# Loads and stores issued by GpSimd, one batch transposed on TensorE, and corrected DMA times in the plan of a fused attention and MLP kernel

## The chip, the cores and the metric

The kernel runs on one core of a Trainium2 chip. The metric is the time on the device in microseconds (us), the median of several runs.

Engines are named as the profile names them: PE is TensorE's matmul stream and PEld its weight loads, DVE is VectorE, ACT is ScalarE, POOL is GpSimd, SP is SyncE. A "q" after a name (SPq, POOLq) means that engine's instruction queue, here the issuing of DMAs. The "granted clock" is the share of TensorE's full clock that the chip allowed in a stretch (1.00 is all of it). PSUM is the memory that TensorE writes its results to; it is used in banks, and to "evict" a bank is to copy it out so that TensorE can write it again. "L301" is line 301 of the kernel; the change adds three lines, so L298 before is L301 after.

## The reference

Eight batches of cosine-weighted linear attention (8 heads, 576 tokens, head width 64), then a two-layer MLP with the gate h·cos(h) on all 4608 tokens:

```python
def phi(x, c, s):
    r = np.maximum(x, 0.0)
    return np.concatenate([r * c, r * s], axis=-1)
q_p = phi(q, cos_w, sin_w)
k_p = phi(k, cos_w, sin_w)
kv  = np.einsum('bhsf,bhsd->bhfd', k_p, v)
z   = np.sum(k_p, axis=2)
num = np.einsum('bhsf,bhfd->bhsd', q_p, kv)
den = np.einsum('bhsf,bhf->bhs', q_p, z)[..., None] + 1e-06
x   = num / den            # then to tokens x 512
h   = x @ w_in             # 512 -> 2048
out = (h * np.cos(h)) @ w_out   # 2048 -> 512
```

## The kernel before

The kernel records every operation as a step of a `Plan`: engine, occupied time, latency, the data it reads and writes. A list scheduler then runs the plan once with these assumed times and emits the steps in order of their planned start. The numbers in the plan thus set the order of each engine's instructions; the engines themselves run them in the order given. A DMA's assumed time is its bytes over a rate, on one shared "wire":

```python
nbytes, rate = s["dma"]
begin = max(free[e] + 1.3, wire)
wire = begin + nbytes / rate
done[n] = wire + 0.7
...
return [st[n] for n in sorted(order, key=lambda n: (st[n]["start"], n))]
```

Each batch is loaded with six DMAs, all issued by SyncE, into one raw tile per input:

```python
def load(b, nm, due, hs=(slice(0, H),)):
    ...
        def go5(h=h, five=five):
            nc.sync.dma_start(out=blocks(m, n)[:, h], in_=five)
        def go4(h=h, four=four):
            nc.sync.dma_start(out=blocks(m, 1 - n)[:, h, 0:NT, :], in_=four)
        pl.add("SP", 0.62, 0, due, go5, (), [(x, n) for x in part],
               dma=(nb * (NT + 1) / 1e3, 330.0))
        # ... and the same for go4
```

The "preps" turn raw q and k into relu(x)·cos on DVE and relu(x)·sin on ACT. There is one buffer `qp`, with one slot for each of five token tiles. From batch 2 on a DMA transpose, issued by SyncE, reads each slot and writes `qT`; the prep of the next batch may overwrite the slot only when that transpose has read it. The attention result x goes the same way (`xT<-x`). Batches 0 and 1 are transposed on TensorE (`q_pe`, `x_pe`).

```python
qp = sb("qp", [P, NT + 1, H, 2, D])        # one buffer, no second copy
...
def q_dma(b, t, due):
    dst, dkey = qdst(b, t)
    pl.add("SP", 0.62, 0, due, lambda: nc.sync.dma_start(
        out=dst, in_=qp[:, t].rearrange("p h g d -> p (h g d)"), transpose=True),
        [("qp", t, g, h) for g in range(2) for h in range(H)], [dkey],
        dma=(262.0, 200.0))
```

The MLP runs per chunk of 512 tokens: layer 1 into four PSUM banks (`M1`), the gate on ACT (`ch`) and DVE (`gT`), layer 2 into two banks (`M2`), evicted by ACT into `ost`, then stored:

```python
act(0.5, due, lambda O=O, t=t, m=m: nc.scalar.activation(
    out=O[:, t % 2, :], in_=M2[m], func=AF.Copy), [("M2", m)], [("ost", o, t % 2, 0)])
...
def put(dst, s, keys, q=nc.sync, eng="SP", nb=256.0):
    pl.add(eng, 0.62, 0, due + 1.0, lambda: q.dma_start(out=dst, in_=s), keys, [],
           dma=(nb, 330.0))
```

The main loop weaves a batch's attention between the layers of the chunk before it:

```python
for c in range(2, NC):
    if c < B:
        attention(c)
    layer2(c - 1)
    layer1(c)
```

## Time and profile before

| | before |
|---|---|
| median time | 351.63 us (3 runs, 350.76 to 352.52); 351.75 with the later run |
| span of the profiled run, granted clock | 348.6 us, 0.992 |
| PE busy | 292.8 us |
| PE idle in 68–204 us | about 22 us |
| DMA transposes of q, issue to landing | median 3.5, longest 7.0 us |

The page of the kernel before, its parts 1 and 4. Part 1 is busy time, share of the span and instruction count for each engine; part 4 is the chain of work that ended last, by engine and by line.

```profile
span 348.6 us, 5319 instructions
...
PE 292.8 (84%) x2032; PEld 154.1 (44%) x2032; DVE 181.0 (52%) x387; ACT 179.2 (51%) x290; POOL 7.9 (2%) x19
...
PE 57%; ACT 19%; DVE 12%; issue 6%; DMA 4%; SPq 0%; DVEq 0%; ACTq 0%
PE M L436 28%; PE M L412 20%; ACT ch L368 10%; DVE gT L370 10%; PE M L395 5%; DMA qm<-in_q_dram 4%; ACT ost L448 4%; ACT qp L233 2%; PE ATT L257 2%; PE ATT L319 1%; DVE x L329 1%; ACT V L246 1%; PE M L288 1%; ACT kp L233 1%; ACT qT L292 0%
```

PE is the busiest engine and holds most of the chain. DMA has 4% of it, two loads of q that start at 3.6 and 60.5 us.

The waits of PE in the kernel before, from 60 to 205 us: what ended the idle time, us in total, times, longest.

```profile
PE M L412 <- DVE gT L370: 9.0, 14, 1.3
PE M L395 <- DVE gT L370: 4.2, 3, 2.0
PE M L436 <- ACT ost L448: 3.9, 6, 0.7
...
```

PE's waits are short: a PSUM bank that the gate has not freed, or (L436) layer 2 waiting for an eviction, never over 0.7 us.

The instructions of line L298 (the DMA transposes of q) in the kernel before: issue duration in ns as min/median/max, then the time from issue to landing.

```profile
L298 SPq DMA_TRANSPOSE qT<-qp x30: 1232/1259/4068, 70.9 to 229.8; - x30
...
DMA to landing us min/median/max: 3.0/3.5/7.0
```

SyncE's timeline in the kernel before, a part of 143 to 160 us: start, duration, what was issued.

```profile
143.75 0.67 SPq L213 DMA_DIRECT2D km<-in_k_dram  x1
144.51 1.26 SPq L358 DMA_TRANSPOSE xT<-x  x1
145.94 3.76 SPq L298 DMA_TRANSPOSE qT<-qp  x2
...
```

Loads and transposes stand in one queue, one after another, with hardly a pause. That crowding is what the change sets out to relieve.

### The profile page before, as it was taken

The page shows a single profiled execution, that of the slowest core. Times are in us where ns is not written, and L with a number is a line of the kernel's source. Part 1 is how long each engine was busy: PE and PEld are TensorE (multiplying, and loading weights), DVE is VectorE, ACT ScalarE, POOL GpSimd, SP SyncE. Part 2 cuts the span into 40 slices and gives each one's busy share as a digit, 9 for nine tenths or more (in the row PEclk, how much of TensorE's full clock was granted, in tenths as well). Part 3 has the DMA queues.
Part 4 walks back from the last instruction along what each step waited for, and adds up shares of the span by engine and source line. Part 5 has one row for each costly group of instructions (what it writes and reads, how often), then busy time and mean ns, then how long its engine had stood idle before and what let it go on. Part 6 is the DMA issues. An engine that isn't in the chain of part 4 may idle for free.

```text
span 348.6 us, 5319 instructions
## 1 busy us (share of the span) xinstructions
PE 292.8 (84%) x2032; PEld 154.1 (44%) x2032; DVE 181.0 (52%) x387; ACT 179.2 (51%) x290; POOL 7.9 (2%) x19
## 2 busy tenths in 40 slices
PE   0478899676888779878988998999999999999983
PEld 0466646565543335433433453545444444444331
DVE  2646546967844667566666663643464333333300
ACT  2845558777553664564755665344433443443311
POOL 0430000000000000000000000000000000000000
PEclk9989999999999999999999999999999999999998
DMA  6999958999999989798494641561041010101111
GB/s 211 246 224 210 220 194 275 318 286 222 227 223 273 330 141 280 232 208 203 135 270 137 107 107 30 127 116 60 1 117 68 16 60 0 62 0 60 60 62 60
DMA packets 80217, 53.87 MB, mean 155 GB/s; under 512 B 48832, under 2 KB 77760, under 8 KB 80192
## 3 DMA queue, kind: packets, MB, share of 16 engines
q1 hardware_dynamic: 75520, 49.17, 53.3%
q0 software_dynamic: 4224, 4.19, 7.3%
q8 instruction: 16, 0.26, 0.3%
q10 hardware_dynamic: 448, 0.17, 0.2%
q14 instruction: 9, 0.07, 0.1%
HBM read 36.74 MB, written 9.44 MB: 132 GB/s over the span
## 4 chain that ended last, share of the span: by engine, by line
PE 57%; ACT 19%; DVE 12%; issue 6%; DMA 4%; SPq 0%; DVEq 0%; ACTq 0%
PE M L436 28%; PE M L412 20%; ACT ch L368 10%; DVE gT L370 10%; PE M L395 5%; DMA qm<-in_q_dram 4%; ACT ost L448 4%; ACT qp L233 2%; PE ATT L257 2%; PE ATT L319 1%; DVE x L329 1%; ACT V L246 1%; PE M L288 1%; ACT kp L233 1%; ACT qT L292 0%
## 5 line engine op out<-in xcount | busy, mean ns | idle before, releaser
L370 DVE TENSOR_TENSOR gT<-M,ch 128x512 f16<-128x512 f32 x144 | 98.2, 690 | 110.1 <-ACT ch L368 53.9
L368 ACT ACTIVATE ch<-M,PIH 128x512 f32<-128x512 f32 x144 | 96.6, 686 | 112.5 <-DVE gT L370 83.3
L436 PE MATMUL M<-w_out_sb,gT 128*128 128x512 f16 x576 | 141.0, 379 | 11.4 <-ACT ost L448 10.9
L412 PE MATMUL M<-xT,w_in_sb 128*128 128x512 f16 x384 | 94.7, 378 | 11.7 <-DVE gT L370 9.0
L436 PEld LDWEIGHTS <-gT 128*128 128x128 f16 x576 | 54.6, 97 | 76.7 <-issue 18.1
L412 PEld LDWEIGHTS <-w_in_sb 128*128 128x128 f16 x448 | 43.2, 97 | 68.2 <-issue 21.1
L395 PE MATMUL M<-xT,w_in_sb 128*128 128x256 f16 x256 | 30.4, 272 | 8.3 <-DVE gT L370 6.5
L448 ACT ACTIVATE ost<-M 128x512 f32<-128x512 f32 x35 | 20.6, 592 | 32.1 <-PE M L436 32.1
L395 PEld LDWEIGHTS <-w_in_sb 128*128 128x128 f16 x256 | 24.6, 97 | 13.1 <-issue 6.8
L233 ACT ACTIVATE kp<-km,CS 128x512 f16<-128x512 f32 x40 | 26.2, 712 | 4.9 <-DMA km<-in_k_dram 4.9
L233 ACT ACTIVATE qp<-qm,CS 128x512 f16<-128x512 f32 x39 | 26.2, 713 | 2.7 <-DMA qm<-in_q_dram 2.7
L236 DVE TENSOR_SCALAR kp<-km,CS 128x512 f16<-128x512 f32 x40 | 16.6, 481 | 11.3 <-DMA km<-in_k_dram 6.7
L329 DVE TENSOR_TENSOR x<-ATT,rec 128x512 f16<-128x512 f32 x30 | 20.6, 688 | 0.6
L319 PEld LDWEIGHTS <-qT 128*128 128x128 f16 x320 | 15.0, 101 | 10.1 <-issue 4.5
L236 DVE TENSOR_SCALAR qp<-qm,CS 128x512 f16<-128x512 f32 x41 | 18.1, 476 | 1.8 <-DMA qm<-in_q_dram 1.8
L288 PE MATMUL M<-IDENT,qp 128*128 128x128 f16 x72 | 6.3, 258 | 12.2 <-ACT qp L233 12.2
L412 PE MATMUL M<-xR,w_in_sb 128*128 128x512 f16 x64 | 16.4, 379 | 0.0
L319 PE MATMUL ATT<-kvz,qT 128*128 128x65 f16 x272 | 13.7, 195 | 2.0 <-DVE x L329 2.0
L249 DVE CAST V<-vm 128x512 f16<-128x512 f32 (+1 forms) x42 | 14.2, 382 | 0.0
L257 PE MATMUL ATT<-V,kp 128*128 128x65 f16 x320 | 11.8, 194 | 1.7 <-DVE V L249 1.0
L257 PEld LDWEIGHTS <-kp 128*128 128x128 f16 x320 | 11.1, 98 | 3.8 <-DVE V L249 1.2
L288 PEld LDWEIGHTS <-qp 128*128 128x128 f16 x80 | 6.2, 117 | 13.0 <-ACT qp L233 12.4
(38 smaller groups left out, 58.7 us busy)
## 6 DMA issues: line engine op xcount, KB each, us to landing
out_dram<-ost SPq DMA_DIRECT2D x32, 256.0 KB, 2.8
km<-in_k_dram SPq DMA_DIRECT2D x8, 640.0 KB, 5.3
qm<-in_q_dram SPq DMA_DIRECT2D x8, 640.0 KB, 5.7
km<-in_k_dram SPq DMA_DIRECT2D x8, 512.0 KB, 6.1
qm<-in_q_dram SPq DMA_DIRECT2D x8, 512.0 KB, 6.7
vm<-in_v_dram SPq DMA_DIRECT2D x6, 640.0 KB, 4.9
vm<-in_v_dram SPq DMA_DIRECT2D x6, 512.0 KB, 5.9
w_in_sb<-in_moe_w_in_dram POOLq DMA_DIRECT2D x4, 512.0 KB, 9.4
```

Of the source, the lines that this page charges most:

```text
L233: act(0.2 + 0.37 * f, due, lambda: nc.scalar.activation(out=out_, in_=in_, func=AF.Relu, scale=sc), rd, wr)
L236: dve(0.09 + 0.28 * f, due, lambda: nc.vector.tensor_scalar(out=out_, in0=in_, scalar1=0.0, scalar2=sc, op0=ALU.max, op1=ALU.mult), rd, wr)
L257: nc.tensor.matmul(ATT[:, hb, hh * D1:(hh + 1) * D1], lhsT=kp[:, t, h].rearrange("p g d -> p (g d)"), rhs=V1[b % 2][:, t, h, :], start=(t ...
L288: nc.tensor.matmul(ps[:, h, :], lhsT=qp[:, t, h].rearrange("p g d -> p (g d)"), rhs=IDENT, is_transpose=True)
L319: nc.tensor.matmul(A[:, hb, hh * D1:(hh + 1) * D1], lhsT=a[:, h, :], rhs=z[:, h, :], start=(i == 0), stop=(i == len(parts) - 1))
L329: dve(0.62, due, lambda: nc.vector.tensor_tensor(out=x16[n].rearrange("p (b h) d -> p b h d", b=2), in0=N[:, :, :, 0:D], in1=rec[n].rearra ...
L368: act(0.59, due, lambda: nc.scalar.activation(out=ch[c], in_=bank, func=AF.Sin, bias=PIH, scale=1.0), [key, "PIH"], [("ch", c)])
L370: dve(0.61, due, lambda: nc.vector.tensor_tensor(out=dst, in0=bank if len(dst.shape) == 2 else bank.rearrange("p (j s) -> p j s", j=dst.sh ...
L395: nc.tensor.matmul(M1[m][:, jj * 2 * P:(jj + 1) * 2 * P], lhsT=w_in_sb[:, cc, j * P:(j + 1) * P], rhs=X[:, cc, ts], start=(cc == 0), stop= ...
L412: nc.tensor.matmul(M1[m], lhsT=w_in_sb[:, cc, j * P:(j + 1) * P], rhs=X[:, cc, :], start=(cc == 0), stop=(cc == NCT - 1))
L436: nc.tensor.matmul(M2[m], lhsT=G[:, j, t * P:(t + 1) * P], rhs=w_out_sb[:, j, :], start=(j == 0), stop=(j == NJT - 1))
L448: act(0.5, due, lambda O=O, t=t, m=m: nc.scalar.activation(out=O[:, t % 2, :], in_=M2[m], func=AF.Copy), [("M2", m)], [("ost", o, t % 2, 0)])
```

## The change

The intent: give SyncE only the DMA transposes, let the mostly idle GpSimd (busy 7.9 of 348.6 us) issue loads and stores from batch 2 on, take the transposes of batch 2 (and x of batch 3) from the DMA engines, and put the measured durations of transposes and loads into the plan. The core of the diff, with cuts:

```diff
+    Q_PE, X_PE = (2,), (2, 3)
...
-            def go5(h=h, five=five):
-                nc.sync.dma_start(out=blocks(m, n)[:, h], in_=five)
+            queue, eng, occ = (nc.sync, "SP", 0.65) if b < 2 else (nc.gpsimd, "POOL", 0.95)
+
+            def go5(h=h, five=five, queue=queue):
+                queue.dma_start(out=blocks(m, n)[:, h], in_=five)
...
-            pl.add("SP", 0.62, 0, due, go5, (), [(x, n) for x in part],
-                   dma=(nb * (NT + 1) / 1e3, 330.0))
+            pl.add(eng, occ, 0, due, go5, (), [(x, n) for x in part],
+                   dma=(nb * (NT + 1) / 1e3, 310.0))
...
-        pl.add("SP", 0.62, 0, due, lambda: nc.sync.dma_start(      # q_dma
+        pl.add("SP", 1.25, 0, due, lambda: nc.sync.dma_start(
...
-            dma=(262.0, 200.0))
+            dma=(262.0, 160.0))
...
-            [("x16", n)], [dkey], dma=(131.0, 200.0))               # x_dma, occupied 0.62 -> 1.25 too
+            [("x16", n)], [dkey], dma=(131.0, 140.0))
...
-            def put(dst, s, keys, q=nc.sync, eng="SP", nb=256.0):
-                pl.add(eng, 0.62, 0, due + 1.0, lambda: q.dma_start(out=dst, in_=s), keys, [],
+            def put(dst, s, keys, q=nc.gpsimd, eng="POOL", nb=256.0):
+                pl.add(eng, 0.95, 0, due + 1.0, lambda: q.dma_start(out=dst, in_=s), keys, [],
...
+            elif b in Q_PE:
+                q_pe(b, t, ATT[:, t % 2, :], ("ATT", t % 2), "ACT" if t % 2 else "DVE", tt + 1)
             else:
                 q_dma(b, t, tt + 1)
...
-                x_dma(b, t, n, tt + 1)
+                if b in X_PE:
+                    x_pe(b, t, n, ATT[:, t % 2, :], ("ATT", t % 2), "ACT", tt)
+                else:
+                    x_dma(b, t, n, tt + 1)
```

## The prediction

> **What bounds the kernel now.** TensorE, in an order fixed at build time: the busy table has PE at 292.8 of 348.6 us, granted clock 0.992. By the windows view, 0 to 68 us loses much to start-up; from 68 to 204 us PE idles 22 us (7.1 in 68-108, 6.7 in 108-144, 4.9 in 144-176, 3.3 in 176-204); from 204 us it is dense.
>
> The waits view says what those 22 us are: layer 1 waiting for a PSUM bank that the gate (cosine on ScalarE, multiply on VectorE, 0.69 us each) has not freed, 9 us as "L412 <- DVE gT" after 90 us and 4.7 us in batch 1's half-width layer 1; eviction of layer 2, 0.69 us each time; x from VectorE, 2 us. No PE wait there is for a DMA; ScalarE and VectorE wait for loads only 3.6 us between 60 and 210 us.
>
> SyncE's queue is crowded: between 68 and 136 us it issues almost without pause (DMA transposes 1.25 us, up to 4.07; loads 0.6 us). But nothing on the chain of waits waits for it after 68 us, so freeing it should by itself win almost nothing.
>
> **What the change does.**
> - 36 loads and most stores go to GpSimd at about 0.78 us each (weight loads: 3.12 us for four). Bytes and DMA engines stay the same; the Trainium skill, "DMA: Bandwidth & Descriptors", section "Issuing engines are not separate DMA queues", says this only saves issue time. Expected: transposes issue near 1.25 us and land within 3.5 us.
> - "SBUF — State Buffer", section "Who interferes with whom", warns of a port shared by GpSimd and VectorE's two-port modes. The weight loads hardly overlap preps, so this trace doesn't show it; I expect below 1 us on the path.
> - Five q tiles and nine x tiles (batches 2 and 3) move to TensorE: 76 transposes at 0.055-0.06 us, an estimated +4.4 us of PE, about 2 of it filling stalls in batch 1's layer 1; ScalarE +7.4 us (2 x 1.02, 9 x 0.59), VectorE +2.1 us, both with slack, though each sits in front of a gate.
> - The corrected DMA times reorder the static program. In the order listing, layer-1 groups directly following another layer-1 group, where the gate binds (roughly 0.3 us each in this trace), number 15, 13, 9, 0 for chunks 2 to 5 before and 10, 6, 13, 5 after: 37 against 34. Chunks 2 and 3 gain 3-4 us, chunks 4 and 5 lose 2.5-3. From chunk 6 on the order is the same.
>
> Sum: +4.4 of work, -2 hidden in batch 1's stalls, -1 from fewer bunched groups, -2 to -3 from a less crowded order on the other engines: about -1.
>
> **Predicted: 350.5 us, 80% range 343 to 357; faster by over 2% 0.25, within 2% 0.65, slower by over 2% 0.10.**
>
> **What would show it.** PE busy about 297 us; PE idle in 68-108 down to 5 us; chunk 3's layer 1 almost free of gate waits, chunk 4's with 4 us; SyncE idle for much of 68-200 us; transposes near 1.25 us; the stretch from chunk 6 on unchanged.
>
> **What would make it wrong.** Faster: if SyncE's late issues delayed preps enough to shape the gate's queues, or if fewer transposes relieve the DMA engines (mean share near 1.0 until 150 us): then 340-344. Slower: if GpSimd's descriptor writing and the preps block each other, if a store at the head of GpSimd's queue holds back loads, or if the ATT bank's chain (numerator, divide, transpose, evict) stalls PE for each tile.

## The result, and the profile after

| | before | after |
|---|---|---|
| median time, us | 351.75 (350.76 to 352.52, 4 runs) | 375.76 (374.8 to 379.23, 4 runs) |
| ratio to before, 95% interval | | 1.0702 (1.0628 to 1.0776): slower |
| profiled span, us; granted clock | 348.6; 0.992 | 373.7; 0.965 |
| PE busy, us | 292.8 | 303.2 |

Ratios here and below are the mean time of one kernel's fast runs over that of the other's of the same rounds, so they are not quite the ratio of the medians that are quoted. Executions over 1.5% slower than the fastest of the same kernel are left out of the means. The results were correct.

The page of the kernel after, the same parts as before.

```profile
span 373.7 us, 5465 instructions
...
PE 303.2 (81%) x2108; PEld 162.2 (43%) x2108; DVE 183.1 (49%) x390; ACT 185.9 (50%) x301; POOL 54.9 (15%) x93
...
PE 53%; ACT 16%; DVE 14%; DMA 11%; issue 5%; SPq 0%; DVEq 0%; POOL 0%; ACTq 0%
PE M L439 25%; PE M L415 17%; DVE gT L373 8%; DMA qT<-qp 8%; ACT ch L371 7%; PE M L398 4%; ACT ost L451 4%; DMA qm<-in_q_dram 3%; ACT qp L236 2%; PE ATT L260 2%; PE ATT L322 2%; DVE x L332 1%; DVE kp L239 1%; ACT qT L295 1%; PE M L291 1%
```

The new entry is "DMA qT<-qp 8%": a DMA transpose of q now holds 8% of the span on the chain, where it held nothing. Part 4 alone shows what to look for, not why.

The windows view of the kernel after, two stretches: start and end, length, busy us (and instructions) of PE, PEld, DVE, ACT and POOL, then granted clock, DMA share and GB/s.

```profile
179.00:196.00 17.00, 0.39 (x9) 0.30 (x8) 1.89 (x6) 2.42 (x4) 0.00 (x0) 0.65 1.31 169
196.00:203.00 7.00, 6.72 (x28) 2.83 (x28) 3.92 (x11) 0.95 (x2) 1.21 (x2) 0.64 1.15 200
```

For 17 us every compute engine stands almost still. Packets are under way on the DMA engines all the time (a share over 1 means that their times overlap), yet only 169 GB/s are moved. In the next 7 us PE is busy, at a granted clock of 0.64.

PE's longest wait in the kernel after (150 to 206 us):

```profile
PE M L439 <- ACT ost L451: 17.6, 2, 16.9
...
```

PE M L439 is layer 2 waiting for a PSUM bank, and its releaser is ACT's eviction. The kernel before had the same wait, never over 0.7 us. So why did ACT not evict? Its timeline in the kernel after answers:

```profile
180.93 0.72 ACT L236 ACTIVATE qp<-qm,CS 128x512 f16<-128x512 f32 x1 [3.99 <-issue]
186.08 0.72 ACT L236 ACTIVATE qp<-qm,CS 128x512 f16<-128x512 f32 x1 [4.43 <-DMA qT<-qp]
195.02 0.72 ACT L236 ACTIVATE qp<-qm,CS 128x512 f16<-128x512 f32 x1 [8.22 <-DMA qT<-qp]
195.65 0.58 ACT L451 ACTIVATE ost<-M 128x512 f32<-128x512 f32 x1
...
```

The eviction (L451) stands in ACT's queue behind preps of the next batch's q (L236). The last two of these preps wait 4.43 and 8.22 us for DMA transposes that still read their `qp` slots; for the first the view names no releaser. The chain of the kernel after, the part that ends in this wait (start, us, what):

```profile
166.40 28.60 DMA qT<-qp
...
195.02 0.72 ACT qp L236
195.74 0.49 ACT ost L451
...
196.28 3.57 PE M L439 x8
...
```

One transpose takes 28.60 us. The eight matmuls after it take 3.57 us, about 0.45 us each. Eight matmuls at the busy clock take 1.89 us (the same line elsewhere in this trace). The Trainium skill, "TensorE: Matmul & The Clock Gate", section "What's actually happening", states that an idle array falls back to half clock after an idle window of about 3.4 us; this trace agrees: PE stops at about 179 us, and the granted clock is 1.00 from 179 to 184 us and 0.50 from 184 to 201 (the 0.65 and 0.64 above are means over both).

The instructions of line L301 of the kernel after, which are the transposes of q:

```profile
L301 SPq DMA_TRANSPOSE qT<-qp x25: 1231/1324/12777, 102.8 to 255.8; - x25
...
DMA to landing us min/median/max: 3.0/6.1/28.6
```

SyncE's timeline in the kernel after, from 159 us on (start, duration, what was issued):

```profile
159.12 20.06 SPq L301 DMA_TRANSPOSE qT<-qp  x2
179.22 7.86 SPq L361 DMA_TRANSPOSE xT<-x  x2
187.19 7.69 SPq L301 DMA_TRANSPOSE qT<-qp  x1
...
```

SyncE has nothing but transposes to issue, and yet two of them occupy it for 20 us: to landing, the median went from 3.5 to 6.1 us and the longest from 7.0 to 28.6 us.

Where the time went along the span, by PE idle time in stretches that begin and end with the first layer-1 matmul of a chunk:

| stretch of after (us) | PE idle after | the same chunks before |
|---|---|---|
| 0 – 107.9 | 28.3 | 29.2 |
| 107.9 – 141.0 | 4.0 | 6.7 |
| 141.0 – 203.2 | **20.5** | 4.9 |
| 203.2 – 231.9 | 4.7 | 3.3 |

From chunk 6's layer 1 to the end the two kernels need the same: 113.9 us before, 114.3 after. Of the 24 us, about 16 are the extra idle time of one stretch; PE's busy time grew by 10.4 us, and a little is won back in the stretches before. The experiments below split the 10.4: the added transposes alone make it 4.2 more (e3, 297.0), and with the corrected plan as well, but no standstill, it is already 9.1 more (e1, 301.9). The cold clock of the standstill is thus a small part of it: from 184 to 201 us PE is busy only 4.7 us in all.

### The profile page after: what moved, and what is told of

It is laid out like the page before. It is cut to its first block, busy times and chain, and to the rows that moved or that the text cites. A ratio compares the mean times of both kernels' runs of the same rounds, so it can differ in the third digit from the quotient of the medians.

```text
span 373.7 us, 5465 instructions
## 1 busy us (share of the span) xinstructions
PE 303.2 (81%) x2108; PEld 162.2 (43%) x2108; DVE 183.1 (49%) x390; ACT 185.9 (50%) x301; POOL 54.9 (15%) x93
## 4 chain that ended last, share of the span: by engine, by line
PE 53%; ACT 16%; DVE 14%; DMA 11%; issue 5%; SPq 0%; DVEq 0%; POOL 0%; ACTq 0%
PE M L439 25%; PE M L415 17%; DVE gT L373 8%; DMA qT<-qp 8%; ACT ch L371 7%; PE M L398 4%; ACT ost L451 4%; DMA qm<-in_q_dram 3%; ACT qp L236 2%; PE ATT L260 2%; PE ATT L322 2%; DVE x L332 1%; DVE kp L239 1%; ACT qT L295 1%; PE M L291 1%
## 5 line engine op out<-in xcount | busy, mean ns | idle before, releaser
L439 PE MATMUL M<-w_out_sb,gT 128*128 128x512 f16 x576 | 143.3, 383 | 27.2 <-ACT ost L451 26.8
L415 PE MATMUL M<-xT,w_in_sb 128*128 128x512 f16 x384 | 95.3, 378 | 10.4 <-DVE gT L373 7.0
L439 PEld LDWEIGHTS <-gT 128*128 128x128 f16 x576 | 55.0, 98 | 92.3 <-issue 35.6
L462 POOL DMA_DIRECT2D out_dram<-ost x38 | 21.3, 565 | 197.8 <-ACT ost L451 197.8
L398 PE MATMUL M<-xT,w_in_sb 128*128 128x256 f16 x256 | 32.6, 282 | 5.3 <-DVE gT L373 3.3
L451 ACT ACTIVATE ost<-M 128x512 f32<-128x512 f32 x35 | 20.7, 593 | 29.4 <-PE M L439 29.4
L236 ACT ACTIVATE qp<-qm,CS 128x512 f16<-128x512 f32 x39 | 26.2, 717 | 17.8 <-DMA qT<-qp 13.4
L398 PEld LDWEIGHTS <-w_in_sb 128*128 128x128 f16 x256 | 25.2, 101 | 10.7 <-issue 5.6
L236 ACT ACTIVATE kp<-km,CS 128x512 f16<-128x512 f32 x40 | 26.8, 717 | 4.8 <-DMA km<-in_k_dram 4.8
L239 DVE TENSOR_SCALAR kp<-km,CS 128x512 f16<-128x512 f32 x40 | 17.4, 486 | 8.6 <-DMA km<-in_k_dram 5.4
L322 PEld LDWEIGHTS <-qT 128*128 128x128 f16 x320 | 15.8, 105 | 10.4 <-issue 4.0
L260 PE MATMUL ATT<-V,kp 128*128 128x65 f16 x320 | 13.1, 201 | 2.5 <-ACT xR L355 1.1
L291 PEld LDWEIGHTS <-qp 128*128 128x128 f16 x120 | 8.7, 111 | 14.4 <-ACT qp L236 12.3
L322 PE MATMUL ATT<-kvz,qT 128*128 128x65 f16 x272 | 14.3, 199 | 0.5 <-ACT xT L355 0.4
```

The source lines that it names most:

```text
L236: act(0.2 + 0.37 * f, due, lambda: nc.scalar.activation(out=out_, in_=in_, func=AF.Relu, scale=sc), rd, wr)
L239: dve(0.09 + 0.28 * f, due, lambda: nc.vector.tensor_scalar(out=out_, in0=in_, scalar1=0.0, scalar2=sc, op0=ALU.max, op1=ALU.mult), rd, wr)
L260: nc.tensor.matmul(ATT[:, hb, hh * D1:(hh + 1) * D1], lhsT=kp[:, t, h].rearrange("p g d -> p (g d)"), rhs=V1[b % 2][:, t, h, :], start=(t ...
L322: nc.tensor.matmul(A[:, hb, hh * D1:(hh + 1) * D1], lhsT=a[:, h, :], rhs=z[:, h, :], start=(i == 0), stop=(i == len(parts) - 1))
L398: nc.tensor.matmul(M1[m][:, jj * 2 * P:(jj + 1) * 2 * P], lhsT=w_in_sb[:, cc, j * P:(j + 1) * P], rhs=X[:, cc, ts], start=(cc == 0), stop= ...
L415: nc.tensor.matmul(M1[m], lhsT=w_in_sb[:, cc, j * P:(j + 1) * P], rhs=X[:, cc, :], start=(cc == 0), stop=(cc == NCT - 1))
```

## The experiments

The change has three separable parts: (a) who issues loads and stores, (b) the plan's numbers and with them the order, (c) the TensorE transposes. The theories, with the letters that the texts use where they use one:

- **Q, queue sharing:** loads on another engine's queue share the DMA engines with the transposes differently from loads ahead of them in SyncE's queue, and a transpose gets the worse part.
- **O, order:** the corrected plan put preps ahead of evictions in such a way that the kernel stands still, whoever issues.
- **H, head of queue:** a store that waits at the head of GpSimd's queue holds loads back and lets them loose in a bunch.
- **S, stores:** it is the stores from GpSimd that disturb the transposes.

### e1: everything of the change but GpSimd

The plan keeps the name POOL and its costs, so each engine's order is the changed kernel's; only the queue of the DMAs is SyncE's.

```diff
-            queue, eng, occ = (nc.sync, "SP", 0.65) if b < 2 else (nc.gpsimd, "POOL", 0.95)
+            queue, eng, occ = (nc.sync, "SP", 0.65) if b < 2 else (nc.sync, "POOL", 0.95)
-            def put(dst, s, keys, q=nc.gpsimd, eng="POOL", nb=256.0):
+            def put(dst, s, keys, q=nc.sync, eng="POOL", nb=256.0):
```

> The plan, the program order and the TensorE transposes of the changed kernel are kept; only the engine that issues loads and stores is SyncE again. Theory Q (two queues): the 17 us in which TensorE stands still at 179 us come from DMA transposes on SyncE's queue and loads on GpSimd's queue running at the same time, each slowing the other. Then the stall goes: about 353 to 358 us (375.8 less 17 of stall and about 3 of slow matmuls after it, with 4.4 of added TensorE work left), and no transpose takes over 12 us to land. Theory O (order): the corrected times bunch three loads and the transposes in front of the prep instructions whatever queue they are on. Then it stays above 368 us.

Measured: 356.72 us, ratio 1.0129 (1.0087 to 1.0172), before 352.35 in the same rounds. The transposes (line L301 of this kernel):

```profile
L301 SPq DMA_TRANSPOSE qT<-qp x25: 1232/1559/4837, 103.6 to 238.8; - x25
...
DMA to landing us min/median/max: 3.1/4.7/8.4
```

and PE's waits in this kernel:

```profile
PE M L439 <- ACT ost L451: 10.3, 21, 0.7
...
```

As theory Q expected, the eviction waits are 0.7 us at most again with the same order, and no transpose takes over 8.4 us. O falls: the order alone does not stop the kernel. Some 19 us belong to the issuing engine, and 4.4 us to the plan and the TensorE tiles together.

### e2: the old order, GpSimd issues

```diff
+            queue = nc.sync if b < 2 else nc.gpsimd      # loads; plan unchanged
-            def put(dst, s, keys, q=nc.sync, eng="SP", nb=256.0):
+            def put(dst, s, keys, q=nc.gpsimd, eng="SP", nb=256.0):
```

(The two half-tile stores at the very end are issued by ACT and SyncE, as in the changed kernel. All transposes from batch 2 on are DMA transposes.)

> The plan, order and DMA transposes of the kernel before; only loads and stores from batch 2 on are issued by GpSimd. Theory Q: with the batch 2 transposes still on DMA there is more to collide, so 360 us or more, with transposes that take over 12 us to land and waits of ScalarE and VectorE for qT. Theory O: 350 to 354 us, as before.

Measured: 373.27 us over the three fast runs (374.62 with the slow one), ratio 1.0604 (1.0528 to 1.068). PE's longest wait here:

```profile
PE M L414 <- DMA xT<-x: 17.3, 1, 17.3
...
```

The old order loses 21 us as well. The victim is another one (layer 1 waits for x, not layer 2 for an eviction), but it is again a DMA transpose, and the longest transpose of q takes 28.3 us.

### e3: TensorE transposes alone

```diff
+    Q_PE, X_PE = (2,), (2, 3)          # and the q_pe and x_pe branches; all else as before
```

> The kernel before with only batch 2's q tiles and the x tiles of batches 2 and 3 transposed on TensorE; old DMA times in the plan, SyncE issues all. Theories Q and O both say no collapse: 349 to 356 us, with about 4.4 us more of TensorE work, partly hidden. If instead the shared ATT bank or the evictions cost much, over 358 us.

Measured: 348.80 us, ratio 0.9917 (0.9862 to 0.9973). That is just below the expected range, and the interval lies below 1, though the gain is under 2%. PE busy is 297.0 us, as predicted for the whole change. The added work at least pays for itself.

### e4: the corrected plan alone

e1 with no added TensorE transposes.

```diff
-    Q_PE, X_PE = (2,), (2, 3)
+    Q_PE, X_PE = (), ()
```

> The changed kernel's plan (its DMA times and its engine names) with every transpose left on DMA and SyncE issuing all. The order-kept run was 1.3 per cent slower than before, the TensorE tiles alone 0.8 per cent faster. If the two parts add up, the corrected plan is what costs: 358 to 362 us. If they do not, and the cost of the order-kept run was the 4.4 us of TensorE work, this is 350 to 354 us.

Measured: 363.09 us, ratio 1.0333 (1.0275 to 1.0391), before 352.38. That is just above the expected 358 to 362. The corrected plan by itself **costs** 10.7 us. With the same 2032 matmuls PE is busy 299.0 us in place of 292.8: from 70 to 80 us the granted clock is 0.73 here (0.76 after, 0.78 in e1), where it is 1.00 before and in e3. The TensorE tiles then win 6.4 us on this plan (e1 against e4), against 3.5 us on the old one (e3).

### e5 and e6: which of GpSimd's DMAs does it

e5 is the changed kernel with its loads issued by SyncE and its stores by GpSimd; e6 is the reverse.

```diff
 e5:  queue of loads  nc.gpsimd -> nc.sync     (stores stay on GpSimd)
 e6:  queue of stores nc.gpsimd -> nc.sync     (loads stay on GpSimd)
```

> The changed kernel's order; stores issued by GpSimd, loads by SyncE. Theory Q (sharing by packets: while loads and transposes are on two queues, each 256-byte transpose packet is served once for each 4 to 5 KB load packet): stores are a fifth of the traffic and come alone, so 355 to 361 us, no wait of ScalarE for qT over 4 us. Theory S (a store at the head of GpSimd's queue is what delays things, or the stores themselves block the transposes): most of the 17 us stall stays, above 365 us.

> The changed kernel's order; loads issued by GpSimd, stores by SyncE. Theory Q: a stall of 10 us or more stays, 365 to 378 us. Theory H (head of the queue: in the changed kernel the loads of k, q and v came bunched at 157 us because a store before them had waited 18.9 us; without the store they spread and meet the transposes one at a time): 354 to 360 us.

Measured: e5 355.92 us, ratio 1.0108 (1.0058 to 1.0158); e6 378.41 us, ratio 1.0761 (1.0692 to 1.083). PE's waits in e6:

```profile
PE M L439 <- ACT ost L451: 27.8, 21, 17.9
...
```

e5 is as fast as e1, so S falls: the stores are harmless. e6 has the whole loss (378.41, just above Q's range) though no store stands in GpSimd's queue, so H falls too. It is the loads on GpSimd. (No run of the kernel put the loads on ScalarE's queue, so whether any second queue does it there stays untested; m1 tries it outside the kernel.)

### m1: transposes and loads by themselves

This kernel gives a wrong result on purpose. It runs phases with a fence between them (VectorE reads everything the phase wrote): ten DMA transposes of a 128x1024 tile from SyncE, eight loads (640 or 512 KB), or both, with the loads from different engines.

```python
for phase in range(8):
    T = phase not in (1, 3)
    Q = {0: None, 1: nc.gpsimd, 2: nc.gpsimd, 3: nc.sync, 4: nc.sync, 5: nc.scalar,
         6: nc.gpsimd, 7: None}[phase]
    for n in range(NTR):
        if Q is not None and n < len(loads):
            ld(*loads[n], Q)
        if T:
            tp(n)                      # DMA transpose, always from SyncE
    fence()
```

> Gives a wrong result on purpose. Eight phases, each fenced from the next: ten q-tile transposes alone; eight loads (4.7 MB) alone from GpSimd; both at once (transposes SyncE, loads GpSimd); loads alone from SyncE; both on SyncE's queue in turn; transposes SyncE with loads ScalarE; transposes SyncE with loads GpSimd again; transposes alone. Theory Q: the two phases with GpSimd take clearly longer than the sum of the two alone (about 14 us for the transposes, 16 to 18 us for the loads), and both on one queue takes about the sum, 30 to 34 us. Theory O: together takes no more than the sum on either queue. The ScalarE phase tells whether any second queue does it or only GpSimd's.

Measured (one run):

| phase | us for all | longest transpose, us |
|---|---|---|
| transposes alone | 15.9, at the end again 15.5 | |
| loads alone, GpSimd / SyncE | 16.5 / 16.6 | |
| both, loads from GpSimd | 31.2, again 30.5 | 20.0, again 19.6 |
| both, all from SyncE | 30.6 | 8.0 |
| both, loads from ScalarE | 29.8 | 12.2 |

The windows view of m1 (columns: start and end, length, DVE and POOL busy, clock, DMA share, GB/s): both with loads from GpSimd, then both from SyncE.

```profile
53.30:84.50 31.20, 2.44 (x22) 5.43 (x8) 1.00 1.00 235
...
102.40:133.00 30.60, 2.38 (x26) 0.00 (x0) 1.00 1.07 240
...
```

Expected by Q was a total clearly longer than the sum of the two alone; that **missed**: 31.2 us against 15.9 + 16.5 = 32.4. By the words on record this result is O's; it is e1 that speaks against O, and Q lives on in a changed form. Nothing is lost in total. What changes is who waits. With loads in a second queue, a single transpose takes up to 20.0 us where it takes at most 8.0 us in one queue, and the loads are held up much less (they end after 21.1 us instead of 16.5).

Why the split is so uneven shows in the DMA view of m1, two slices of 2 us. First transposes alone (24 to 26 us; kind, packets, MB, share of the DMA engines' time):

```profile
q1 hardware_dynamic: 1487, 0.37, 97.8%
...
```

Then both, loads from GpSimd (64 to 66 us), q0 being GpSimd's loads and q1 the transposes:

```profile
q0 software_dynamic: 167, 0.68, 95.4%
q1 hardware_dynamic: 167, 0.04, 10.0%
...
```

The two queues got the **same number of packets**, 167 and 167, and with it 0.68 against 0.04 MB. (Over 62 to 70 us it is 602 and 601; before, while the first loads get going, and after, the transposes get more.) A transpose moves in packets of 256 bytes (0.37 MB over 1487), a load from GpSimd in packets of 4096 or 5120 bytes. One packet in turn thus gives the transposes about a seventeenth of the bytes: 167 packets in the time in which they alone get 1487. A transpose of a q tile needs 1024 packets, so at this rate it stands until most of the waiting loads are through. This agrees with the Trainium skill, "DMA: Bandwidth & Descriptors", section "Queues, rings and completion order", which states that each DMA engine goes round between queues that have work, a packet at a time.

From SyncE's queue the loads go in packets of 1280 and 1024 bytes. The 8.0 us there would fit a queue served in order, where a transpose waits for the loads ahead of it and not for those issued later; that is argued, not shown packet by packet. From ScalarE's queue (12.2 us, packets of 1280 and 1024 bytes too) it lies between.

### m2, m3 and m4: can the loss of throughput be made outside the kernel?

The kernel shows one thing that m1 does not. The DMA view of the kernel after, 155 to 200 us:

```profile
DMA packets 9034, 8.00 MB, mean 178 GB/s; under 512 B 7664, under 2 KB 7664, under 8 KB 9032
...
q1 hardware_dynamic: 7456, 1.84, 59.1%
q0 software_dynamic: 1576, 6.13, 52.6%
...
```

Packets are under way throughout and move 178 GB/s, where m1 holds 235 to 246 with both kinds at work. In the worst slices of 2 us only 16 to 32 load packets and 87 to 91 transpose packets pass. There the transposes' packets take 200 to 300 ns each, and 18 to 21 in a quiet stretch. While the long transpose is in flight, 165 to 195 us, the picture differs from m1's:

```profile
q1 hardware_dynamic: 2988, 0.74, 68.5%
q0 software_dynamic: 1042, 4.11, 52.1%
...
```

A packet of the transposes takes 110 ns on average (68.5% of 16 engines' 30 us over 2988). In m1 it takes 21 ns alone and 19 ns beside loads (62 to 70 us). The loads suffer too: they move 137 GB/s (4.11 MB in 30 us) against 312 in m1 (2.50 MB from 62 to 70 us), and the six issued from about 157 to 163 us take 7.8 to 22.8 us to land. So turns by packet are not the whole of the 28.6 us: packets that take longer and a lower rate have a part in it. Three more kernels (wrong results on purpose, one run each) tried to make this by itself. m2 adds the smaller x transposes and stores; m3 adds transposes that VectorE's writes release one by one ("paced") and six loads into only 8 partitions ahead of the rest ("skewed", meant to let some DMA engines lag; the trace does not record which engine moved a packet, so whether they did is not shown); m4 interleaves ten such small loads with the others.

```python
# m2:  x transposes | x + loads | q,x | q,x + loads | stores | q + stores | q,x + loads + stores | all SyncE
# m3:  q + loads | paced | skewed | all SyncE | q,x paced + skewed + loads + stores | paced, all SyncE
# m4:  q + loads | small loads | small + loads | q + small | q + small + loads | all SyncE
```

> Gives a wrong result on purpose. Eight fenced phases: ten x-tile transposes alone; with eight GpSimd loads; five q and five x tiles alone; with eight GpSimd loads; eight stores alone from GpSimd; ten q tiles with eight GpSimd stores; q, x, loads and stores, loads and stores from GpSimd; the same all on SyncE. In the first micro run the time together was no more than the sum of the times alone (31.3 against 32.6 us); in the changed kernel the DMA engines moved only some 140 GB/s of loads while transposes waited. If x tiles or stores next to loads are what makes that loss, some phase here takes over 1.25 times the sum of its parts. If all phases take about their sum, the loss in the kernel comes from something else, and stays open.

> Gives a wrong result on purpose. In the kernel the DMA engines lost throughput while both queues were busy; in the two micro runs they did not. Six fenced phases: control (ten q tiles, eight GpSimd loads); the same with each transpose paced by a VectorE write of its source; the same with six small loads to 8 partitions put ahead[...]; all on SyncE; q, x, loads and stores paced and lagging; q, x, loads and stores on SyncE. If lagging engines are what loses throughput, the third phase takes over 1.2 times the control (31 us); if pacing is, the second. If none does, the loss stays open.

> Gives a wrong result on purpose. [...] Six fenced phases: ten q transposes with eight GpSimd loads (31 us before); ten small loads alone; small and eight normal loads; transposes with small loads; transposes with both kinds, from GpSimd; the same all on SyncE. If engines out of step are what loses throughput when transposes and loads are on two queues, the fifth phase takes over 1.25 times the sum of transposes (16), loads (16.5) and small loads alone, or the fourth over 1.25 times its sum, and the sixth does not. If all stay below, the loss stays open.

Measured in m2: x alone 14.3 us, with GpSimd loads 24.2; q and x with loads 28.7 (alone 14.5); eight stores alone 7.4, q with GpSimd stores 22.9; all kinds 31.8 from GpSimd and 30.9 from SyncE. The longest transpose was 21.7 us with GpSimd's loads and stores and 7.1 us with everything from SyncE. No phase takes over 1.25 times the sum of its parts. In m3 the plain phase took 31.9 us, paced 28.2, skewed 36.2, all from SyncE 28.5. Skewed is 1.13 times the plain one, under the threshold set, though some 10 us within it, while the small loads run, showed the low rates of the kernel (77 GB/s); the fifth phase, with everything from GpSimd, took 39.0. In m4 small loads with the others took 32.1 us (parts 33.8), with transposes about 30 (parts 33.3), all three from GpSimd about 47 (parts about 50) against about 40 from SyncE. None passed its threshold. **What lowers the rate in the kernel stays open.** The starving of single transposes, up to some 20 us, is reproduced by itself in m1, m2 and m3.

### e7, e8, e9: what in the corrected plan costs time

All three are built on e3 or before, with loads and stores on SyncE.

```diff
 e7:  e3 + transposes planned with occupied 0.62 -> 1.25, q rate 200 -> 160, x rate 200 -> 140
 e8:  e3 + loads planned with rate 330 -> 310
 e9:  before + Q_PE, X_PE = (2,), ()          # q tiles of batch 2 only
```

> The kernel with the TensorE tiles alone (348.8 us), and of the corrected DMA times only those of the transposes. The order listing has 20 bunched layer-1 groups against 24 without, and TensorE's work is the same. If the transposes' times are what made the corrected plan cost 10.7 us: 354 us or more. If it is the loads' times or the engine names: 345 to 349 us.

> The kernel with the TensorE tiles alone (348.8 us), and of the corrected DMA times only the loads' rate, 310 for 330. In every kernel that has the whole corrected plan, batch 1's layer 1 starts at 72.4 us rather than 67.8. If the loads' rate alone does that: first layer-1 matmul of batch 1 at about 72 us and 351 to 356 us. If not: 347 to 350 us and 67.8 us.

> The kernel before with only batch 2's five q tiles on TensorE; all x tiles stay on DMA, old plan times, SyncE issues. Order listing: 20 bunched layer-1 groups against 37 before and 24 with the x tiles too; added TensorE work about 2.2 us against 4.4. If bunched groups cost 0.5 us each, as the TensorE-tiles run implies, this is about 346 us (344 to 348). If the x tiles on DMA come too late for the denser order, it is 350 us or more, with waits of layer 1 for xT.

| kernel | median us | ratio (95%) |
|---|---|---|
| e7 | 350.88 | 0.9954 (0.9922 to 0.9986) |
| e8 | 352.00 | 0.9997 (0.9958 to 1.0035) |
| e9 | 347.04 | 0.9865 (0.9809 to 0.992) |
| before, same rounds | 352.57 | |

Against e3's 348.80, the corrected transpose times cost 2.1 us and the corrected load rate 3.2 us by the medians; the intervals of e7 and e8 overlap that of e3 (0.9862 to 0.9973), so neither is clear of the noise. e7 fell between the two expectations and settles neither. The whole corrected plan with the same tiles (e1) costs 7.9 us over e3, so the two do not quite make it up; the rest must come with the changed engine names and costs of loads and stores in the plan, which was not run by itself. One visible part: the first layer-1 matmul of batch 1 comes at 67.77 us before, 67.68 in e3, 68.83 in e7, 69.43 in e8 (about 72 was expected), 71.53 in e1, 72.41 in e4 and 72.47 after. The corrected plan delays the start of the dense part by up to 4.7 us. The low granted clock at 70 to 80 us comes with it in e4, e1 and after, but also in the profiled run of e9 (0.80, start at 69.57), so what it costs is open.

The prediction counted bunched layer-1 groups (a group directly behind another, where the gate binds). Counted in the plan's order, with attention work between them left out, they number 37 before, 24 in e3, 20 in e9, 20 in e7, 25 in e8, 34 in e1 and after, 48 in e4. The count goes with the time for e3, e9 and e4, but e7, with e9's count, is 3.8 us slower. It is no reliable predictor.

e9 has the lowest median, below both the kernel before and the changed one. Its interval lies below 1, but the gain is under 2%, and it overlaps that of e3, so the two cannot be told apart.

### e10: GpSimd issues, but no DMA transposes for it to disturb

```diff
-    Q_PE, X_PE = (2,), (2, 3)
+    Q_PE, X_PE = tuple(range(2, 8)), tuple(range(2, 8))
```

> The changed kernel, loads and stores still from GpSimd, but every q and x tile from batch 2 on is transposed on TensorE, so that apart from one x tile no DMA transpose is left to meet a load. TensorE has 15 us more work than in the changed kernel, and 21 bunched groups for 34. Theory Q: the standstill of TensorE is gone (no wait of TensorE over 3 us after 70 us), loads of 640 KB land in about 5 us each as they do alone, and the time is about 362 to 368 us in spite of the work. If GpSimd's loads by themselves cause the standstill: a wait over 8 us remains and it is 380 us or more.

Measured: 374.30 us, ratio 1.0643 (1.0601 to 1.0684), before 351.78. PE's waits in e10, from 70 us to the end:

```profile
PE M L439 <- ACT ost L451: 7.4, 15, 0.7
PE ATT L291 <- ACT qT L295: 6.9, 10, 1.3
...
PE M L398 <- ACT ch L371: 1.6, 1, 1.6
...
```

The standstill is gone: no wait is over 1.6 us. The 640 KB loads from GpSimd land in 4.6 to 5.4 us (medians of the three inputs). So the loads from GpSimd do no harm by themselves; it takes both, loads in another queue and DMA transposes beside them. The time missed its expectation of 362 to 368 us, as the further transposes on TensorE cost more than expected: the span is 370.5 us against e1's 355.1, 15.4 us more. PE is busy 316.1 us against 301.9 in e1. That PE had few stalls left for this work to fill past batch 2 would explain it; no run shows it by itself.

## Why the prediction was wrong, point by point

The prediction said 350.5 us, in 343 to 357; measured was 375.76. By the medians of the experiments, the 24.0 us are:

| term | predicted | measured | from |
|---|---|---|---|
| GpSimd issues loads and stores | 0 ("only saves issue time"), below 1 for the port | +19.6 | 24.0 less e1's 4.4 |
| corrected plan, new order | −1 and −2 to −3 | +10.7 | e4 less before |
| transposes on TensorE | +4.4 −2 | −6.4 (−3.5 on the old plan) | e1 less e4; e3 less before |
| sum | about −1 | +23.9 | |

1. **The step that failed:** "Bytes and DMA engines stay the same … this only saves issue time. Expected: transposes issue near 1.25 us and land within 3.5 us." Measured: issue up to 12.8 us, landing median 6.1 and longest 28.6 us. e1, e5 and e6 put this on the loads' queue; m1 shows, outside the kernel, how a transpose can starve there. The prediction took one section of a page of the skill and not the other one on the same page about turns by packet; together with the packet sizes they say the opposite of "nothing changes". Those sizes were only partly to be seen beforehand: the trace before has transposes in packets of 256 bytes, but from GpSimd only weight loads, in packets of 1024. Bytes and engines stayed the same; **the order in which waiting bytes are served did not** (m1), and in the kernel the packets took longer as well.
2. **The path to PE was not seen either.** The prediction treated DMA transposes as off the path, because no PE wait before was for a DMA. True at 3.5 us of landing. But `qp` has one buffer, the next batch's preps wait for the transpose, and the evictions of layer 2 stand behind those preps in ACT's queue. At 28.6 us that slack is used up, and PE's wait then names ACT, not the DMA.
3. **The corrected plan was mis-sized, with the wrong sign:** +10.7 us in place of a gain of 3 to 4. A closer model of DMA times did not give a better order here. Part of it is the later start of batch 1's layer 1 (72.41 us in e4 against 67.77), and PE's busy time grew by 6.2 us with the same matmuls, at a granted clock of 0.73 from 70 to 80 us; the shares, and the rest, are open.
4. **The TensorE transposes were mis-sized, with the wrong sign of the net:** PE's added time was right (e3 has 297.0 us busy, predicted about 297), but what it freed was worth more than the 2 us assumed.
5. **Right, or nearly:** the stretch from chunk 6 on (113.9 and 114.3 us); the stretch of chunk 2 (idle 6.7 to 4.0 us); SyncE idle for part of the time until the transposes back up. PE idle in 68–108 us was predicted at 5 and was 6.5 us (40 less 33.54 busy). PE busy for the whole change was predicted at about 297 and was 303.2, which is a miss: e1, with no standstill, already has 301.9.
6. **The rival worries:** "a store at the head of GpSimd's queue" fell with e6. The port shared by GpSimd and VectorE left hardly a trace: the VectorE preps of q took 485 ns in place of 476, those of k 486 in place of 481. The range's upper end, 357, would have held e1 (356.72), the change without GpSimd's queue.

What is shown: that the loads' queue costs some 19 us, and that it does so through slow DMA transposes (e1, e2, e5, e6, e10); that, outside the kernel, a transpose starves to 20 us beside loads from GpSimd (m1 to m3), with equal numbers of small and large packets served (m1). What is only argued: how much of the kernel's 28.6 us this makes up. It is not all: in the kernel the transposes' packets themselves take longer (110 ns against 19 to 21 in m1) and the total rate falls (178 GB/s); the cause of both stays open.

## What to carry to other kernels

Before a DMA is moved to another engine's queue, ask what it stood *behind* in the old one: a queue can order bytes as well as issue slots, and in m1 transfers of small packets beside a second queue of large ones got turns, not bytes: the longest grew from 4.0 us alone to 20.0 at no loss of total rate. Follow each such latency to the buffers it holds (here one `qp` buffer) and to what stands behind their next writer in an in-order engine. And change one of a plan's inputs at a time: of the three parts here, a piece of the smallest one alone (the q tiles of one batch on TensorE) had the lowest median, 347.04 us, not to be told apart from the whole of that part (e3, 348.80).

## What the Trainium skill lacked or had wrong

- "DMA: Bandwidth & Descriptors", section "Issuing engines are not separate DMA queues", says that issuing from several engines only saves sequencer time. In these runs it changed how the DMA engines were shared: the same loads in the same planned order cost 378.41 us from GpSimd (e6) and 356.72 from SyncE (e1).
- The same page, section "Queues, rings and completion order", has the turns by packet, and m1 agrees (167 and 167 packets in 2 us), but no page draws the consequence or has the packet sizes by kind and issuer: 256 bytes for a transpose, 1024 and 1280 for these loads from SyncE, 4096 and 5120 for the same loads from GpSimd. A 262 KB transpose then took up to 20.0 us in place of 8.0.
- The same page, section "SWDGE vs HWDGE vs iDMA", gives a packet as preferably at most 4096 bytes; the loads issued by GpSimd ran in packets of 5120 bytes too.
- The same page, section "Rules for kernel authors", says, in a row about corrupted results, that a transpose next to ordinary DMAs needs nothing. For the result that held; for time it did not (28.6 us to landing beside GpSimd's loads, 8.4 beside the same loads on SyncE's queue).
- No page has the fall of the total rate in the kernel, 178 GB/s with packets under way throughout, against 235 to 246 in m1; its cause is open here too.
